# One written order of single-engine pieces in place of two lists and due times: retention, Fourier mixing and a feed-forward block on one NeuronCore

## Chip, cores and metric

The kernel runs on 1 core of one Trainium2 chip. The metric is device time in microseconds (us) of one execution, median of several runs. Three runs of the kernel before took 242.15, 242.26 and 242.28 us.

The core has five engines with a queue of instructions each: TensorE (PE, with its weight loads shown apart as PEld), VectorE (DVE), ScalarE (ACT), GpSimd (POOL) and SyncE (SP). Each engine issues its queue in order. DMA transfers are issued from SP, from POOL (where they also change the type) and now and then from ACT.

## What is computed

Inputs are q, k and v of 4 batches, 8 heads, 768 positions and 64 columns, and two weights of 512 x 2048 and 2048 x 512, all float32.

```python
for t in range(S):                       # retention, per head, with decay gamma
    state = gamma * state + outer(k[t], v[t])
    y[t] = scale * q[t] @ state
x = y, heads side by side                # 768 x 512 per batch
mixed = real(fft(fft(x, axis=1), axis=2))
u = x + mixed
un = (u - mean(u)) / sqrt(var(u) + 1e-6)
out = u + relu(un @ w_ch1) @ w_ch2
```

## The kernel before

**Stages of a batch.** The 768 positions are cut into 6 chunks of 128, the 8 heads into 4 pairs (order 0, 1, 3, 2). For each pair q, k and v (384 KB each) are loaded by SP (L209) into one of 11 input buffers, cast to float16 (L193 and L194 are the helper that records casts and scalings of the first batch; L413 to L428 in later batches), and q and k are transposed: on PE for batches 0 and 1 (products with the identity, L468 and L578, whose results ACT or DVE evict, L584 and L589), by DMA for batches 2 and 3. Then come the scores of each chunk (L492, L622), their masking and decay on DVE (L501, L625), the chunk states (products L516 and L641; the recurrence over the chunks is one scan on DVE in batch 0, L525, and multiply-adds after it, L651), and the outputs (L538 and L548, L672 and L676), which ACT evicts as x (L684).

The real part of the two-dimensional Fourier transform is made by products with cosine and sine tables, folded by their symmetry: DVE adds and subtracts halves (L703, L713), PE does the first axis (L760, L782, L800, L895), ACT and DVE evict g (L767, L771), PE does the second axis (L924, L952, L1006). DVE and POOL add x and the mirrored part to get u (L959 to L991, L1030, L1038), DVE makes the statistics (L1055), ACT the normed un (L1060). un is transposed, either on PE with an eviction (L1105, L1109) or by DMA from SP (L1101). The first product of the feed-forward block writes hidden tiles (L1118, L1135, L1199), relu is their eviction on ACT or DVE (L1122, L1124, L1204), the second product (L1157) is added to u by DVE (L1161) and stored by SP (L1164). In the last batch the second product is made of seven smaller ones of combined blocks (L1270).

The tables are computed on the chip at the start (PE L340 and L343, ACT L359 to L367). The two weights come in four pieces each, w10 to w13 and w20 to w23, 512 KB of float16 each, as casting DMAs on POOL (L1311, L1318).

**What sets the order.** Every step is a Python closure, a unit, with a short name: `k20` casts the first part of pair 2's k, `ae201` masks scores, `sc3` is pair 3's scan, `w10` starts a weight's DMA, `h01` is a hidden product of the first block. Many units of the later batches issue instructions on several engines; for example a transposing unit holds the products of q, their evictions, the products of k and theirs. The order of batch 0's first part is written by hand in the strings FIRST and SECOND. Behind them, `emit` spreads the units of the other work by due times: each stream of units has a start and an end in units of a batch (constants such as DM0, TS0, LD0, HT0), and the units are issued in the order of the times so found.

`pin()` ties each new instruction to the one before it on the same engine, so that the tool that schedules the program keeps that order. It is called for all engines in FIRST, SECOND, in the very first due times and in the last batch. For the rest of batch 0's stretch only POOL's order is pinned, and between them the scheduler may choose. `behind()` and `held()` keep some casts in turn. `late_consts` makes eight scaled copies of the mask on ACT behind one of the first norms.

```python
for e in ev:
    e[3]()
    if e[0] < 1.0:
        behind()
        pin(None if e[0] < 0.05 else ["Pool", "GpSimd"])
    elif e[0] > B - 1:
        pin()
```

A filler (`f512`, L189) is a PE product of zeros, 128 x 512, whose result nobody reads. Eight stand ahead of everything; FIRST holds two more. The loads of batch 0 are issued as q0 k0 v0 q1 k1 v1 q2 k2 q3 k3 v2 v3 at the start, and the weights' DMAs stand in FIRST from `w10`, behind `ae200`, to `w23`. The loads of batch 1 wait for the seventh weight's DMA and a hidden product, those of later batches for score products of the batch before.

Of the kernel before, what the change touches and what calls it, by code (L numbers as in the profile page):

```python
# [18 lines left out]
P = 128  # L19
B, H, S, D = 4, 8, 768, 64  # L20
DM = 512
# [11 lines left out]
DM0, DM1 = (0.120, 0.208, 0.265, 0.344), (0.004, 0.137, 0.232, 0.341)  # L33
TS0 = (0.249, 0.368, 0.406, 0.410, 0.479, 0.544, 0.680, 0.685)
TS1 = (-0.040, -0.020, 0.048, 0.585)
DA0, DA1 = (0.068, 0.080, 0.173, 0.203, 0.292, 0.326), (0.063, 0.067, 0.063, 0.158, 0.168, 0.189)
LD0, LD1 = (0.172, 0.226), (-0.370, 0.140)
HT0 = (0.655, 0.675, 0.673, 0.628)
NPE = 2
LOADS = "q0 k0 v0 q1 k1 v1 q2 k2 q3 k3 v2 v3"  # L40
# [9 lines left out]
FIRST = """  # L50
par qz0 hid hid5 gk3 q0 nid0 ta0 gk1 ta1 gk0 tq0 nid1 gk2 tn0 k00 eq0 tb0 si0 k01 v00 tk0 tn1 ab0
ek00 tb1 co0 ta3 q1 am01 tn3 ab1 am00 tb3 si1 ae000 si3 ta2 ab3 ae010 kv0 co1 ae011 yi00 tn2 sc0
co3 tb2 ab2 tq1 ae001 k10 si2 eq1 k11 co2 nsp tk1 ek10 yi01 v10 yx0 q2 am10 x01 kv1 ae100 am11 x00
sc1 tq2 k20 k21 q3 ae111 eq2 tk2 ae110 tq3 ek20 k30 ae101 am20 am21 ae200 w10 ae201 k31 ae211 yi10
yi11 ae210 yx1 tk3 w11 x10 ek30 eq3 ek31 ta4 w12 tn4 x11 am30 v30 tb4 am31 v20 ae300 stx01 fs0a
w13 si4 f512 kv2 fs0b ab4 yi20 ae301 yi21 co4 cdh0 sc2 v31 s1s10 w20 ae310 yx2 kv3 ae311 x20 s1s00
w21 sc3 x21 yi30 w22 fla yi31 yx3 flb cdh1 x31 w23 fd0 x30 xn1 f512 s1m0 fhb xn0 xm1 stx3 px1 fha
gc00a g0a fd1 s1s11 qe1 xm0 gr0 s1s01 xm2 s1m1 gc11b gc01a xmb gc11a stg00 xe gc01b gc10a stx4 gr3
stg01 g0b gr2 s21 g0c stg10 mu1 qn1 mu2 s22 ul1 stg11 qn2 uu1 stx2 ul2 ste1 gr1 un1 ste0 uu2 xl2
s23 qz1 s20 xu2 qn3 s25 ul3 qn0  # L60
"""
EARLY = (1,)
SECOND = """
h00 un2 ul0 xl3 uu0 xl0 ut1 uu3 h01 xu0 qn5 uu5 s24 xu3 ul5 h10 qn4 un3 xu5 h11 ul4 xl5 uu4 xl4
h12 xu4 ut2 h03 un4 h13 h22 h21 h23 h20 h02
"""
MIX3 = ((0.005, 0.085, 0.110, 0.125, 0.150), (0.190, 0.290, 0.310, 0.325, 0.350),
        (0.345, 0.415, 0.435, 0.460, 0.500))
WS = (0.6, 0.97)
H3_ACT = (0, 1, 2, 3, 5, 6, 7)  # L70
PROD = ((1, 4, 5, 2, 6, 7, 3), (1, 4, 6, 7, 5, 2, 3))
HS_AT = {3: (0, 4), 7: (4, 8)}
# [4 lines left out]
def kernel(  # L77
# [76 lines left out]
    def behind():  # L154
        for x in tc.nc.cur_bb.bb.instructions[mark[0]:]:
            if str(x.engine) in base:
                tc.add_manual_dep(x, base[str(x.engine)],
                                  mybir.DependencyInfo(mybir.DependencyClass.NoSync,
                                                       mybir.DependencyReason.DATA),
                                  reason="behind the first batch")  # L160

    def held(unit):
        def run():
            ins = tc.nc.cur_bb.bb.instructions
            n0 = len(ins)
            unit()
            for n in range(n0, len(ins)):
                m = n - 1
                while m >= 0 and ins[m].engine != ins[n].engine:
                    m -= 1  # L170
                if m >= 0:
                    tc.add_manual_dep(ins[n], ins[m].name,
                                      mybir.DependencyInfo(mybir.DependencyClass.NoSync,
                                                           mybir.DependencyReason.DATA),
                                      reason="casts in turn")
        return run

# [19 lines left out]
    in_of, a_of = {}, {}  # L197
# [3 lines left out]
    def load_unit(b, i, after=None, names="qkv"):  # L201
        def run():
            h0 = 2 * PAIR_ORDER[i]
            for name in names:
                src = srcs[name]
                t = inp.tile([P, 2, NCH, D], f32, tag="in32", name=f"{name}32")
                rows = "h (p c) d -> p h c d" if b < NPE and name == "q" else \
                    "h (c p) d -> p h c d"
                dma = nc.sync.dma_start(t, src[b, h0:h0 + 2].rearrange(rows, p=P))  # L209
                if after is not None:  # L210
                    for x in (w_dma[after].ins, lb[0]["mm"].ins):
                        tc.add_manual_dep(dma.ins, x.name,
                                          mybir.DependencyInfo(mybir.DependencyClass.Sync,
                                                               mybir.DependencyReason.DATA),
                                          reason="loads in turn")
                if b > 1:
                    tc.add_manual_dep(dma.ins, a_of[b - 1, 1].ins.name,
                                      mybir.DependencyInfo(mybir.DependencyClass.Sync,
                                                           mybir.DependencyReason.DATA),
                                      reason="loads behind the transposes")  # L220
                in_of[name, b, i] = t
        return run

    for n in LOADS.split():
        load_unit(0, int(n[1]), names=n[0])()
# [59 lines left out]
    def late_consts():  # L285
        with tc.issue_after(lb[0]["una"].ins):
            for h in range(H):
                nc.scalar.activation(maskp[:, h // 2, h % 2], maskf, AF.Copy, bias=0.0,
                                     scale=float(gam[h] ** (-P)))
# [17 lines left out]
    def pad_unit():  # L307
        for j in range(2):
            nc.vector.memset(qzs[j][:, 0, :, D:P], 0.0)
            nc.vector.memset(qzs[j][:, 1, :, 0:D], 0.0)  # L310

    def qt_zeros():
        for j in range(2):
            nc.vector.memset(qts[j][0:D, 1], 0.0)
            nc.vector.memset(qts[j][D:P, 0], 0.0)
# [85 lines left out]
    def cast_unit(b, i):  # L401
        def run():
            h0 = 2 * PAIR_ORDER[i]
            q32, k32, v32 = (in_of.pop((n, b, i)) for n in "qkv")
            kd = kp.tile([P, NCH, 2, D], f16, tag="kd16", name="kd16")
            v16 = vp.tile([P, NCH, 2, D], f16, tag="v16", name="v16")
            with ExitStack() as es:
                if b < NPE:
                    if (b, i - 1) in last_cast:
                        es.enter_context(tc.issue_after(last_cast[b, i - 1].ins))  # L410
                    q16 = qzs[i % 2].rearrange("p h c d -> p (h c d)")[
                        :, 0:NCH * P].rearrange("p (c h d) -> p c h d", c=NCH, h=2)
                    es.enter_context(tc.issue_after(nc.gpsimd.tensor_scalar(  # L413
                        out=q16, in0=q32.rearrange("p h c d -> p c h d"), scalar1=1.0,
                        scalar2=1.0, op0=ALU.mult, op1=ALU.mult).ins))
                else:
                    q16 = qzs[i % 2]
                    for h2 in range(2):
                        dst = q16[:, h2, :, D * h2:D * h2 + D]
                        nc.gpsimd.tensor_scalar(out=dst, in0=q32[:, h2], scalar1=1.0,  # L420
                                                scalar2=1.0, op0=ALU.mult, op1=ALU.mult)
                for h2 in range(2):
                    kc = nc.gpsimd.tensor_scalar(out=kd[:, :, h2, :], in0=k32[:, h2],  # L423
                                                 scalar1=gkd[:, h0 + h2:h0 + h2 + 1],
                                                 scalar2=1.0, op0=ALU.mult, op1=ALU.mult)
                    if b < NPE:
                        es.enter_context(tc.issue_after(kc.ins))
                last_cast[b, i] = nc.gpsimd.tensor_scalar(  # L428
                    out=v16, in0=v32.rearrange("p h c d -> p c h d"), scalar1=1.0, scalar2=1.0,
                    op0=ALU.mult, op1=ALU.mult)  # L430
            q16_of[b, i], kd_of[b, i], v16_of[b, i] = q16, kd, v16
        return run
# [26 lines left out]
    def t0_unit(i, part):  # L459
        def run():  # L460
            if (0, i) not in at:
                at[0, i] = dict(kT=tp.tile([P, NCH, P], f16, tag="kT", name="kT"),
                                qT=qts[i % 2][:, 0])
# [6 lines left out]

    def te_unit(i, part, n=0):
        def run():
            st = at[0, i]
# [1055 lines left out]
```

## Time and profile before

| What | Value |
|---|---|
| time, median of 3 runs | 242.26 us (242.15 to 242.28) |
| the profiled execution: span from first to last instruction | 240.1 us |
| its time outside the span | the page names none |
| mean granted clock of TensorE | 0.977 |
| PE busy | 231.2 us (96% of the span), 2161 products |
| DVE busy | 189.3 us (79%) |
| ACT busy | 122.2 us (51%) |
| POOL busy | 89.9 us (37%) |
| DMA | 36.41 MB, 152 GB/s on average |

How to read it. A busy time is the sum of the time in which an engine had an instruction under way. PE's products are pipelined, so one that stands in a row of products takes longer from its start to its end than from its start to the next one's start; both are used below and kept apart. In the lines by groups, the columns are the source line, engine, operation, result and inputs, shape and type, count, then busy us and mean ns of one, then the idle time ahead of it and what ended it. In the table of stretches, each engine's busy time stands with its number of instructions, PEclk is the granted clock as a share of full, the DMA share is the sum over queues and can exceed 1. In a timeline the first two columns are start and length in us, and the brackets hold the idle time ahead and its releaser. In the chain of work that ended last, the columns are start, length, and the engine and line. In the slices of the page each digit is a fortieth of the span, 6 us.

### The profile page before, as it was taken

What the parts mean: (1) busy time and instruction counts of PE and PEld (TensorE: products, weight loads), DVE (VectorE), ACT (ScalarE), POOL (GpSimd) and SP (SyncE); (2) the same over time, 40 slices, a digit from 0 to 9 for tenths busy, and PEclk for the clock granted to TensorE, in tenths of its full rate; (3) what the DMA queues carried; (4) which work ended last, traced back from release to release, by engine and by line L of the source; (5) the groups of instructions that cost most, each with busy time, mean ns of one, the idle gap of its engine ahead of it and who ended that gap; (6) DMA issues with size and microseconds to landing.
All of it is one profiled execution on the core that took longest, in us unless ns stands there. A gap on an engine that the chain in (4) does not pass through costs nothing.

```text
span 240.1 us, 5658 instructions
## 1 busy us (share of the span) xinstructions
PE 231.2 (96%) x2161; PEld 159.3 (66%) x2161; DVE 189.3 (79%) x484; ACT 122.2 (51%) x273; POOL 89.9 (37%) x149
## 2 busy tenths in 40 slices
PE   6888899999999999999999999999999999999995
PEld 2465799765765645665567546665567458898884
DVE  7869989877897788996886778899985856777274
ACT  6777775667956345741247423741247316253330
POOL 6667746264400068690000554680000502240302
PEclk9659999999999999999999999999999999999999
DMA  8999999999899647999999558787100141131202
GB/s 175 252 267 195 207 197 201 230 274 248 217 220 215 120 109 164 210 189 144 263 271 212 108 110 227 131 110 171 64 26 0 26 131 44 25 111 25 87 3 87
DMA packets 99466, 36.41 MB, mean 152 GB/s; under 512 B 89840, under 2 KB 96624, under 8 KB 99440
## 3 DMA queue, kind: packets, MB, share of 16 engines
q1 hardware_dynamic: 95072, 31.79, 63.4%
q0 software_dynamic: 4224, 4.19, 10.8%
q8 instruction: 17, 0.28, 0.5%
q14 instruction: 9, 0.07, 0.1%
q10 hardware_dynamic: 144, 0.07, 0.1%
HBM read 27.26 MB, written 6.29 MB: 140 GB/s over the span
## 4 chain that ended last, share of the span: by engine, by line
PE 80%; DVE 6%; ACT 5%; POOL 3%; DMA 2%; issue 2%; SPq 0%; ACTq 0%; POOLq 0%
PE psc L1157 22%; PE psh L1118 19%; PE psh L1199 9%; PE psc L1270 8%; PE psh L1135 4%; PE wkA L622 3%; PE ps L760 3%; PE wkY L676 2%; DMA k<-in_k_dram 2%; PE wkY L672 1%; PE pq L952 1%; ACT qTz L584 1%; PE wkK L641 1%; PE pq L1006 1%; PE tq L468 1%
## 5 line engine op out<-in xcount | busy, mean ns | idle before, releaser
L1157 PE MATMUL psc<-w,ht 128*128 128x512 f16 x288 | 68.5, 379 | 0.0
L1118 PE MATMUL psh<-unT,w 128*128 128x384 f16 x320 | 59.5, 326 | 0.0
L989 POOL TENSOR_TENSOR u<-u,x 128x256 f32<-128x256 f32 x18 | 11.6, 645 | 99.2 <-DVE u L959 98.0
L1157 PEld LDWEIGHTS <-ht 128*128 128x128 f16 x288 | 27.3, 98 | 26.1 <-issue 0.2
L1118 PEld LDWEIGHTS <-w 128*128 128x128 f16 x320 | 29.9, 98 | 16.0 <-issue 0.6
L1122 ACT ACTIVATE ht<-psh 128x384 f16<-128x384 f32 x46 | 22.3, 489 | 23.9 <-PE psh L1118 23.8
L625 DVE TENSOR_TENSOR atm<-wkA,maskp 128x512 f16<-128x512 f32 x36 | 23.9, 685 | 0.7 <-PE wkA L622 0.7
L1199 PE MATMUL psh<-unT,w 128*128 128x256 f16 x192 | 21.5, 272 | 0.0
L1124 DVE TENSOR_SCALAR ht<-psh 128x384 f16<-128x384 f32 x34 | 18.7, 550 | 2.1 <-PE psh L1118 2.0
L1199 PEld LDWEIGHTS <-w 128*128 128x128 f16 x192 | 18.7, 98 | 2.2
L1055 DVE BATCH_NORM_STATS2 bst<-u 128x6 f32<-128x512 f32 x21 | 14.5, 691 | 6.9 <-POOL u L991 6.8
L1204 ACT ACTIVATE ht<-psh 128x512 f16<-128x512 f32 x21 | 12.5, 597 | 12.9 <-PE psh L1199 7.9
L1161 DVE SCALAR_TENSOR_TENSOR ob<-psc,stats,u 128x512 f32<-128x512 f32 x18 | 13.4, 745 | 6.9 <-PE psc L1157 6.7
L651 DVE SCALAR_TENSOR_TENSOR s<-s,gk,wkK 128x128 f16<-128x128 f16 x48 | 16.3, 339 | 1.9 <-ACT s L647 1.3
L684 ACT ACTIVATE x<-wkY,gexp 128x384 f16<-128x384 f32 x24 | 12.8, 581 | 9.7 <-PE wkY L676 9.7
L1060 ACT ACTIVATE un<-u,stats 128x512 f16<-128x512 f32 x15 | 10.8, 720 | 10.7 <-DVE stats L1056 7.7
L423 POOL TENSOR_SCALAR kd<-k,gexp 128x384 f16<-128x384 f32 x24 | 13.9, 588 | 3.1 <-DMA k<-in_k_dram 3.1
L622 PE MATMUL wkA<-qTz,kT 128*128 128x256 f16 x72 | 13.5, 272 | 0.2
L991 POOL TENSOR_TENSOR u<-u,x 128x256 f32<-128x256 f32 x18 | 11.4, 635 | 2.7 <-DVE stats L1056 1.8
L1135 PE MATMUL psh<-unT,w 128*128 128x128 f16 x192 | 11.4, 219 | 0.0
L954 ACT COPY qn<-pq 128x128 f32<-128x128 f32 x18 | 4.9, 274 | 12.4 <-PE pq L952 12.3
L622 PEld LDWEIGHTS <-kT 128*128 128x128 f16 x72 | 6.8, 98 | 6.3 <-ACT kT L589 0.4
(220 smaller groups left out, 432.0 us busy)
## 6 DMA issues: line engine op xcount, KB each, us to landing
q<-in_q_dram SPq DMA_DIRECT2D x16, 384.0 KB, 6.2
k<-in_k_dram SPq DMA_DIRECT2D x16, 384.0 KB, 5.5
v<-in_v_dram SPq DMA_DIRECT2D x16, 384.0 KB, 6.4
out_dram<-ob SPq DMA_DIRECT2D x18, 256.0 KB, 2.8
w<-in_moe_w_ch_dram POOLq DMA_DIRECT2D x8, 512.0 KB, 10.5
out_dram<-o SPq DMA_DIRECT2D x2, 512.0 KB, 2.9
out_dram<-o SPq DMA_DIRECT2D x3, 128.0 KB, 1.7
unT<-un SPq DMA_TRANSPOSE x15, 2.5
```

Source lines behind the costliest of these rows:

```text
L423: kc = nc.gpsimd.tensor_scalar(out=kd[:, :, h2, :], in0=k32[:, h2], scalar1=gkd[:, h0 + h2:h0 + h2 + 1], scalar2=1.0, op0=ALU.mult, op1=AL ...
L622: mm = nc.tensor.matmul(wk[:, c2], st["kT"][:, c, :], st["qT"][:, :, c, :], start=True, stop=True)
L625: nc.vector.tensor_tensor(out=st["atm"][:, 2 * part:2 * part + 2], in0=wk, in1=maskp[:, PAIR_ORDER[i]].unsqueeze(1).to_broadcast([P, 2, 2, ...
L651: nc.vector.scalar_tensor_tensor(out=s16[:, c], in0=s16[:, c - 1], scalar=gk2[:, hp:hp + 1], in1=wk[:, c - c0], op0=ALU.mult, op1=ALU.add)
L1055: nc.vector.bn_stats(bst, u[:, kb, :])
L1118: nc.tensor.matmul(psh, w116[:, cb, fb * P:(fb + 1) * P], unT[:, cb, rt * 384:(rt + 1) * 384], start=(cb == 0), stop=(cb == 3))
L1122: nc.scalar.activation(ht16[:, fb, :], psh, AF.Relu, bias=0.0, scale=-1.0)
L1124: nc.vector.tensor_scalar(out=ht16[:, fb, :], in0=psh, scalar1=-1.0, scalar2=0.0, op0=ALU.mult, op1=ALU.max)
L1135: mm = nc.tensor.matmul(psh[:, f], w116[:, cb, fb * P:(fb + 1) * P], unT[:, cb, kb * P:(kb + 1) * P], start=(cb == 0), stop=(cb == 3))
L1157: nc.tensor.matmul(psc, ht16[:, fb, rb3 * P:(rb3 + 1) * P], w216[:, fb, :], start=(fb == 0), stop=(fb == NFB - 1))
L1199: nc.tensor.matmul(psh[:, t], w116[:, cb, fb * P:(fb + 1) * P], unT[:, cb, p * 256:(p + 1) * 256], start=(cb == 0), stop=(cb == 3))
L1270: nc.tensor.matmul(ps[:, c0:c1], lh(f), rh(f)[:, c0:c1], start=first and f == 0, stop=last and f == 7, skip_group_check=True)
```

## The change

FIRST, SECOND, the due times, `emit`, `behind`, `held` and the many-engine units of later batches go. In their place every unit is cut into pieces that issue on a single engine, and one string, ORDER, of about 1355 names gives the order of all of them, over all four batches:

```diff
-DM0, DM1 = (0.120, 0.208, 0.265, 0.344), (0.004, 0.137, 0.232, 0.341)
...
-LOADS = "q0 k0 v0 q1 k1 v1 q2 k2 q3 k3 v2 v3"
...
-FIRST = """
-par qz0 hid hid5 gk3 q0 nid0 ta0 gk1 ta1 gk0 tq0 nid1 gk2 tn0 k00 eq0 tb0 si0 k01 v00 tk0 tn1 ab0
...
+ORDER = """
+ta1 ta2 nid1 f512 f512 f512 nid0 gk2 lq0 q0 tq0 qtz10 pad11 gk0 lk0 k00 mp6 tn2 tb2 k01 tk0 f512
+gk1 ab2 f512 lv0 v00 qz0 par tn1 lq1 lk1 f512 gk3 f512 si2 lv1 q1 lq2 eq0 ek00 am00 kv0 ae001 k10
+am01 tb1 ab1 k11 tq1 ta3 tn3 ae000 si1 lk2 lq3 v10 ta0 tn0 tb3 ae010 si3 lk3 q2 ab3 tb0 si0 lv2
+f512 f512 f512 tk1 ab0 k21 qtz00 k30 ae011 q3 yi01 w10 sc0 yi00 yx0 eq1 ek10 am11 ae111 x01 tq2
+ae110 am10 ae100 ae101 k20 tk2 eq2 kv1 ek20 am20 sc1 am21 ae211 x00 yi10 yi11 yx1 k31 co1 tk3 x10
+ae210 ae200 ek30 lv3 v20 tq3 eq3 ta4 ae201 tn4 kv2 ek31 hid5 sc2 tb4 am30 f512 ae301 x11 ab4 nsp
+am31 ae300 fs0a fs0b v30 v31 kv3 co4 ae310 w11 si4 yi21 co0 ae311 co3 sc3 yi20 yx2 x20 cdh0 x21
+flb fla fd0 s1s10 yi30 stx01 w12 yi31 yx3 co2 s1s00 s1m0 x30 xn1 stx3 x31 xm0 close fd1 s1m1 fha
+fhb s1s01 g0a hid gc00a s1s11 cdh1 w13 w20 w21 gc10a xmb gc11b stg00 px1 stx4 xn0 mp7 gc01a stg01
...
+1a0_0 1a2_0 1m0_0 1lq2 1tk1 1cv_1 1kv0_1 1m2_0 1s0_1 1s1_0 0h1_5 1s2_1 1cq_2 1tq2 mp2 1ek_1 0h1_3
...
-    for name in FIRST.split():
-        first_of[name]()
-        pin()
...
-    emit(streams)
+    def play(names):
+        for name in names:
+            units[name]()
+            pin()
+
+    units = first_units()
+    pin()
+    play(ORDER.split())
```

The names of a later batch start with its number: `1tk1` transposes k of batch 1's pair 1 on PE, `1ek_1` evicts it, `2dk1` transposes by DMA, `2lk0` loads, `0h1_5` and `0r1_5` are a hidden product and its relu, `0p1_2`, `0o1` and `0st1` are a part of a second product, its addition to u and its store. `pin()` runs behind each piece for all engines, SP and POOL with their DMA queues among them.

Other than the order, three things differ. ORDER holds eleven fillers where FIRST held two, so PE has nine products more; the eight ahead of everything stay. The mask copies of `late_consts` become eight single pieces, `mp0` to `mp7`. And the first weight's DMA waits for the landing of the last load of k in batch 0:

```diff
             w_dma.append(nc.gpsimd.dma_start(
...
+            if g == 0:
+                sync(w_dma[0], load_of["k", 0, 3])
```

In ORDER, `w11` stands behind the casts of the last v (`v30`), and `w12` to `w21` behind a scaling of a table (`cdh0`); on ACT, the cast of pair 2's v (`v20`) stands ahead of the eviction of pair 3's q (`eq3`). The number of instructions on DVE, ACT, POOL and SP is the same in both kernels.

More of the change, by code (lines that the diff above doesn't have):

```diff
@@ L202, in run, with load_piece @@
+    def load_piece(b, i, name):
         def run():
             h0 = 2 * PAIR_ORDER[i]
[L204 to L221, printed above, removed]
@@ L399, with cast_piece @@
     on = dict(x.split(":") for x in ENGINES.split())
-    def cast_unit(b, i):
+    def cast_piece(b, i, what):
         def run():
[L403 to L431, printed above, removed]
@@ new lines, in run, with out3 @@
+            key = ("ps", p, bank_of(p, n), c0)
+            if key not in pr:
+                pr[key] = ps_g.tile([P, 256], f32, tag="g", name="psc", padded_shape=[P, DM])
+            for f in range(f0, f1):
+                nc.tensor.matmul(pr[key][:, c0:c1], lh(f), rh(f)[:, c0:c1],
+                                 start=first and f == 0, stop=last and f == 7,
+                                 skip_group_check=True)
+        return run
+    def out3(p):
+        if "o" not in pr:
+            pr["o"] = up.tile([P, NCH, DM], f32, tag="u32", name="o32")
+        return pr["o"]
```

1023 lines of the change are left out of this document (502 added, 521 removed).

## Prediction

> **What bounds the kernel now.** I read the page's 40 slices first, then a table of stretches, then the chain that ended last inside the two stretches where TensorE (PE) is not full.
>
> ```profile
> PE   6888899999999999999999999999999999999995
> PEclk9659999999999999999999999999999999999999
> PE 80%; DVE 6%; ACT 5%; POOL 3%; DMA 2%; issue 2%; SPq 0%; ACTq 0%; POOLq 0%
> ```
>
> ```profile
> core 0: us, PE busy (x) PEld busy (x) DVE busy (x) ACT busy (x) POOL busy (x), PEclk, DMA share, GB/s
> 0.00:7.50 7.50, 4.92 (x24) 1.97 (x24) 6.09 (x35) 5.16 (x12) 5.17 (x18) 1.00 0.88 192
> 7.50:17.70 10.20, 9.54 (x102) 6.62 (x100) 7.41 (x13) 8.23 (x17) 6.96 (x9) 0.50 1.26 260
> 17.70:30.00 12.30, 10.67 (x167) 8.16 (x165) 11.01 (x29) 9.44 (x23) 8.92 (x13) 1.00 1.24 201
> 30.00:50.00 20.00, 20.00 (x282) 17.20 (x281) 17.84 (x52) 13.66 (x34) 9.47 (x15) 1.00 1.17 218
> 50.00:65.00 15.00, 14.57 (x160) 9.67 (x159) 11.40 (x30) 11.33 (x21) 8.51 (x12) 1.00 1.11 238
> 65.00:85.00 20.00, 19.77 (x183) 12.98 (x182) 16.30 (x41) 11.10 (x23) 0.02 (x1) 1.00 0.94 180
> 85.00:130.00 45.00, 44.55 (x377) 27.66 (x375) 38.39 (x92) 20.25 (x48) 18.90 (x32) 1.00 1.03 200
> 130.00:185.00 55.00, 54.81 (x433) 33.00 (x432) 45.33 (x106) 24.80 (x60) 18.88 (x32) 1.00 0.53 111
> 185.00:237.00 52.00, 52.00 (x451) 41.85 (x450) 35.00 (x90) 18.27 (x43) 13.11 (x18) 1.00 0.18 54
> 237.00:240.10 3.10, 0.32 (x6) 0.14 (x3) 0.56 (x2) 0.00 (x0) 0.00 (x0) 0.91 0.42 137
> ```
>
> PE carries 80% of the chain. It is full from 30 to 50 us and from 185 to 237. So an order of the work can gain in three places only: ahead of 30 us, where PE idles 2.58 + 0.66 + 1.63 = 4.87 us and runs at half clock for 10.2 us; between 50 and 185, where it shows 0.43 + 0.23 + 0.45 + 0.19 = 1.30 us of idle; and in the last 3.1 us, the final eviction and store, which the new order keeps.
>
> The 1.30 us is a lower bound, as a drained pipeline hides its refill behind the last product's modelled end. The chain gives the interval of products in a row:
>
> ```profile
> 48.19 0.22 PE pst L1105 x4
> 48.42 3.88 PE psc L1157 x18
> ...
> 53.15 0.69 ACT qTz L584
> ...
> 57.17 0.81 ACT kT L589
> ```
>
> 3.88 / 18 = 0.216 us for 512 columns, 0.22 / 4 = 0.055 for 128; I take 0.109 for 256 and 0.028 for 64. The products of 51 to 59 us are these:
>
> ```profile
> L1157 PE MATMUL psc<-w,ht 128*128 128x512 f16 x19 | 5.2, 379 | 0.0
> L622 PE MATMUL wkA<-qTz,kT 128*128 128x256 f16 x6 | 1.1, 273 | 0.1
> L641 PE MATMUL wkK<-v,kd 128*128 128x128 f16 x10 | 1.0, 218 | 0.1
> L578 PE MATMUL tq<-ident,q16z 128*128 128x128 f16 x12 | 1.0, 219 | 0.0
> L578 PE MATMUL tq<-ident,kd 128*128 128x128 f16 x12 | 1.0, 218 | 0.2 <-ACT qTz L584 0.2
> L672 PE MATMUL wkY<-s,qTz 128*128 128x64 f16 x10 | 0.6, 193 | 0.0
> ```
>
> With 4 transposes (L1105) and 6 products of L676 more, they need 19 x 0.216 + 6 x 0.109 + 38 x 0.055 + 16 x 0.028 = 7.3 of the 8 us: 0.7 is lost, where the rows show 0.4 of idle. Counted so from the starts of the 1153 products between 50 and 185 us (160 + 183 + 377 + 433 in the table), the loss is about 1.4 us until 65 and 3.3 after it.
>
> **The change part by part.** The page names no time for the profiled execution beside its span of 240.1 us; against the median of 242.26 us, 2.16 us lie around it, and I keep them. Both versions issue the same work on DVE, ACT, POOL and SP; PE gets nine more products. So the terms are waits.
>
> *Nine products without a result.* Their kind in the trace:
>
> ```profile
> L189 PE MATMUL wps<-ht x10: 379/620/634, 1.2 to 26.4; 128*128 128x512 f16 x10
> ```
>
> Warm they cost 9 x 0.216 = 1.9 us of PE; cold, at twice that, 3.9. Ten of the eleven in the new list stand ahead of the third pair's state, where PE idles and waits for loads and casts; I take 0, as the 4.87 us of idle cover them. If that cover goes they cost up to 3.9.
>
> A gain from them would have to come through the clock: at 0.50 the 9.54 us of PE work between 7.5 and 17.7 us would shrink to 4.8 at full clock. The Trainium skill, "TensorE: Matmul & The Clock Gate", section "Part 1: The HAM clock gate", says that the array runs at half rate after an idle window of some 3.4 us and returns to full rate after one busy window. By that rule fillers ahead of 7.5 us keep the clock up. The trace speaks half for it: the clock falls behind a stretch with 2.58 us of idle, but it stays at 0.50 for 10.2 us although PE shows 94% busy. I count no gain from it in the sum, and keep it as a rival.
>
> *First weights behind the third k, the others behind the last v.* The rows ahead of the end of the first batch's attention, on POOL, ACT and DVE, and the bytes of 18.5 to 22.4 us by queue (q0 are POOL's weights):
>
> ```profile
> 18.59 2.46 POOL L1311 DMA_DIRECT2D w<-in_moe_w_ch_dram  x3
> 22.55 0.56 POOL L194 TENSOR_SCALAR v<-v 128x384 f16<-128x384 f32 x1 [1.50 <-DMA v<-in_v_dram]
> ```
> ```profile
> 20.04 0.80 ACT L193 ACTIVATE qTz<-tq 128x768 f16<-128x768 f16 x1
> ...
> 21.19 0.85 ACT L193 ACTIVATE v<-v 128x768 f16<-128x768 f32 x1
> ```
> ```profile
> 23.13 0.81 DVE L525 TENSOR_TENSOR_SCAN s<-gk,wkK 128x320 f16<-128x320 f32 x1
> 23.86 0.99 DVE L501 SCALAR_TENSOR_TENSOR atm<-wkA,maskf 128x384 f16<-128x384 f32 x2
> 24.96 0.82 DVE L525 TENSOR_TENSOR_SCAN s<-gk,wkK 128x320 f16<-128x320 f32 x1
> 25.70 0.61 DVE L703 TENSOR_TENSOR xab<-x 128x390 f16<-128x390 f16 x2
> ...
> 26.78 0.54 DVE L713 TENSOR_TENSOR eo<-xab 128x768 f16<-128x768 f16 x1
> ```
> ```profile
> q1 hardware_dynamic: 1852, 0.47, 72.3%
> q0 software_dynamic: 258, 0.26, 49.0%
> ```
>
> Weights took 0.26 of 0.73 MB while v2 and v3 were under way, 36% of 3.9 us: without them v3 lands 1.4 us earlier, with w10 alone in front about 0.7 earlier, at 21.8. That is not gained whole. On ACT the cast of v2 (0.85) now stands ahead of the eviction of the fourth pair's q (0.80), which before was done at 20.84: with v2 at about 20.4 (its cast started at 21.19 before), that eviction ends at 22.0, 1.2 late, and the fourth pair's masked products on DVE follow it. In exchange DVE's scan of pair 2 comes at 21.6 instead of 23.13. Behind that scan's end at 22.4 the list holds seven DVE pieces: four masked products and two folds at about 0.46 from start to start (two in 0.99 with the last one's tail), and the last scan (0.82), 3.5 us: it ends at 25.9, before at 25.78. Then come the small folds (0.61) and the difference (0.54) at once, where before a table's scaling of 0.6 stood between them: 27.0 instead of 27.32, so the first Fourier products start 0.3 us earlier. Behind them PE's list counts: PE still idles 1.63 us between 17.7 and 30, and the new order brings Fourier products and small transposes of later use into it; of these 1.63 us I take 0.7. **Sum of the start: -1.0 us**, bounds +0.9 (the 1.2 of the late eviction less the 0.3) and -3.0 (all of the 1.63, and v3 with no weights in front, 1.4).
>
> The lower bound comes from the weights. By 30 us the table of stretches has moved 7.5 x 192 + 10.2 x 260 + 12.3 x 201 = 6.6 MB; the twelve loads are 12 x 393 KB = 4.7 of these, so 1.9 MB are weights, and the fourth piece of 0.52 MB has passed near 31 us. The new list asks for it in its second hidden product, some 2 us behind the point where PE is full. It is late next if the start gains 2 or more.
>
> *Batch 1's transposes and evictions, 50 to 65 us.* Before, the chain runs over ACT's evictions from 53.15 to 57.98 (the quoted first and last of six, each 0.7 to 0.8, with a copy between them), with PE short of ready products. The new list puts two hidden products of 16 x 0.055 and three second products of 4 x 0.216 between the transposes of pair 0 and their first use: 1.8 + 2.6 = 4.4 us of PE work over three evictions of 0.8, a copy and a norm of 0.7 (3.3 us). The cover is there, so most of the 1.4 us goes: **-1.0**, bounds 0 and -1.4.
>
> *Everything pinned to single-engine pieces, 65 to 185 us.* An instruction that the scheduler put at a busy engine's tail can now stand where it is wanted; each engine, SP's and POOL's queues too, waits in the written order. No row shows which of 3.3 us stays. I take a bit less than half, **-1.5**; bounds -3.3 and +8 (the slower rival). What is late next are the Fourier folds on DVE (16.30 of 20 us busy in 65 to 85), which feed PE with about 1 us to spare.
>
> *185 us on, and the tail:* PE is full before; 0.
>
> Sum: 240.1 - 1.0 - 1.0 - 1.5 = 236.6 us span, and with 2.16 around it **238.8 us**.
>
> **The rivals.**
>
> *The clock stays up.* Then the start gains its bound of 3.0 instead of 1.0: 238.8 - 2.0 = 236.8 us. For it: the fillers fall into the idle of the first 7.5 us, and the clock falls just behind it. Against it: DVE (11.01 of 12.3 us busy in 17.7 to 30) and the loads pace this part. Chance 0.13.
>
> *Part of it only.* The order trades old waits for new ones of the same size in one half of the kernel: the start gains nothing (late eviction) and the later gaps give 1.2: 241.1 us. Chance 0.12.
>
> *Slower: SP's queue as a line in which all wait.* Where loads, stores and DMA transposes stand in one written order, a load whose buffer is still held, or a store whose result is late, holds the transposes behind it, and PE has nothing else that its own list lets it do.
>
> ```profile
> v<-in_v_dram SPq DMA_DIRECT2D x16, 384.0 KB, 6.4
> ...
> unT<-un SPq DMA_TRANSPOSE x15, 2.5
> ```
>
> Of the 31 transposes on SP in the new list (15 of them the norm's) 15 follow directly on a load or a store, 11 in the old list. If PE stands for 8 of these for about 1 us (2.5 less the cover), 8 us come in. With the start and the stretch until 65 us still gained (-2.0) and no gain in the later part the time is 242.26 - 2.0 + 8 = 248.3 us, with half of that wait 244.3. It decides from 2 us, a quarter of a microsecond per transpose held. I put the case at 244.3. For it: the lists were not free to move when a wait lasts longer than in this trace. Against it: PE has several products between the transposes and their use, and the loads, at a median of 6.4 us, are issued further ahead than that. Chance 0.25.
>
> *The order changes, the time doesn't:* if loads and DVE pace the start and the later waits are data and not order, 242.3 us. Chance 0.05.
>
> **How the numbers follow.** Forecast (238 to 240 us) 0.45, clock 0.13, part 0.12, slower 0.25, same 0.05. Within 0.2% is about what a measurement of this kernel can tell from no change. So faster 0.70, same 0.05, slower 0.25. The range goes from the clock rival with the gaps' full gain in part (236.8 - 1.2 = 235.6) to just short of the slower case's middle, 244.0, which leaves out half of that case (0.13) and some 0.05 below.
>
> **What would show it.** Right: the cast of the last v on POOL starts before 22 us; the last scan on DVE ends near 25.9; the first Fourier products start near 27.0; PE idle between 50 and 65 us under 0.2; no row of waits on PE for the transposed norm. Wrong: a PEclk row without the 5 and 6 (the clock rival); PE idle above 1.3 us between 65 and 185, ended by unT or by folds (the slower one); the fillers at the head of the chain ahead of the first transposes of q; eviction of the fourth q later than 22 us with DVE idle behind it.

## The result and the profile after

The changed kernel takes 239.83 us (median of 6 runs, 239.21 to 241.16); the kernel before took 242.2 us in the same comparison (6 runs, 241.99 to 243.46). The ratio is 0.990, interval 0.988 to 0.993: 1% faster, 2.4 us. The profiled execution took 239.83 us with a span of 238.1 us, 1.7 us around it; before, the span was 240.1 us. So 2.0 us of the gain lie in the span. The rest lies around it: in the executions of the kernel before for which both numbers are listed, 2.0 to 2.2 us stand around the span, in those of the changed kernel 1.7 to 1.8. No run shows what shortened it; the hybrid below, with the old start, has 2.0 to 2.1 again.

The slices of PE and its clock and the shares of the chain, from the page of the changed kernel:

```profile
PE   7777979999999999999999999999999999999994
PEclk9999999999999999999999999999999999999999
PE 83%; DMA 8%; SPq 5%; DVE 1%; issue 1%; POOL 1%; ACT 0%; POOLq 0%
```

The 5 and the 6 of the clock are gone. (The row says nothing of the first 5 us; see a_nofill.) DVE's and ACT's shares of the chain (6% and 5% before) went to 1% and 0%; DMA's rose from 2% to 8%. The table of stretches says where:

```profile
core 0: us, PE busy (x) PEld busy (x) DVE busy (x) ACT busy (x) POOL busy (x), PEclk, DMA share, GB/s
0.00:7.50 7.50, 5.54 (x23) 1.98 (x24) 5.84 (x34) 5.41 (x13) 4.89 (x17) 1.00 0.87 188
7.50:17.70 10.20, 8.08 (x116) 4.94 (x116) 7.59 (x15) 6.52 (x13) 5.05 (x7) 1.00 1.26 260
17.70:30.00 12.30, 10.96 (x173) 8.60 (x168) 11.49 (x31) 10.98 (x25) 8.89 (x13) 1.00 1.08 168
30.00:50.00 20.00, 18.51 (x243) 15.24 (x242) 15.78 (x47) 12.05 (x29) 8.90 (x14) 1.00 1.16 201
50.00:65.00 15.00, 15.00 (x165) 10.78 (x163) 11.86 (x26) 10.66 (x19) 9.44 (x14) 1.00 1.17 241
65.00:85.00 20.00, 20.00 (x215) 14.15 (x214) 17.80 (x45) 13.95 (x32) 4.91 (x10) 1.00 1.27 200
85.00:130.00 45.00, 44.85 (x383) 28.51 (x381) 40.95 (x95) 21.44 (x50) 21.40 (x36) 1.00 1.13 201
130.00:185.00 55.00, 55.00 (x447) 33.89 (x445) 46.78 (x108) 23.61 (x60) 16.05 (x26) 1.00 0.52 106
```

Between 50 and 185 us PE shows 0.15 us of idle instead of 1.30. Between 30 and 50, where it had none, it now shows 1.49. All of that is one wait, the only one of PE's that the view of waits shows behind 25 us:

```profile
PE psh L1128 <- DMA w<-in_moe_w_ch_dram: 1.5, 1, 1.5
```

The table of losses, with one profile of each kernel, counts the loss as the prediction did: from each product's start to the next start, less the interval of its width (0.216 us for 512 columns, 0.162 for 384, 0.109 for 256, 0.056 for 128, 0.029 for 64). "Useful at 35" is the sum of these intervals of the products that started before 35 us, without the fillers of the lists. Each row is one execution; that of the hybrid and that of a_spfree are about 1 us faster than the median of their runs.

| kernel | lost 0-35 | 35-50 | 50-65 | 65-185 | useful at 35 | span |
|---|---|---|---|---|---|---|
| before | 12.5 | 0.0 | 1.4 | 3.3 | 20.8 | 240.1 |
| changed | 11.8 | 0.0 | 0.0 | 1.2 | 19.6 | 238.1 |
| changed, again | 11.1 | 0.0 | 0.0 | 1.3 | 20.3 | 237.5 |
| a_nofill | 14.1 | 0.4 | 0.0 | 1.6 | 19.3 | 239.1 |
| a_h03 | 10.6 | 0.5 | 0.7 | 1.8 | 20.9 | 238.6 |
| a_h03_nofill | 14.6 | 0.4 | 0.0 | 1.3 | 18.7 | 239.6 |
| b_fill | 12.4 | 0.0 | 1.3 | 3.9 | 19.1 | 242.4 |
| a_wearly | 12.2 | 0.0 | 0.0 | 1.3 | 19.3 | 238.5 |
| a_wearly_h03 | 12.0 | 0.5 | 0.0 | 1.5 | 19.4 | 239.1 |
| a_w2 | 10.9 | 0.0 | 0.0 | 1.0 | 20.5 | 237.0 |
| a_w2_h03 | 10.9 | 0.4 | 0.0 | 2.3 | 20.5 | 238.7 |
| hybrid | 13.0 | 0.7 | 0.5 | 0.9 | 20.3 | 237.9 |
| a_spfree | 11.1 | 0.0 | 0.0 | 1.9 | 20.3 | 238.0 |
| a_free | 11.2 | 0.0 | 2.6 | 5.6 | 20.2 | 246.7 |

So from before to changed: behind 50 us 3.5 us are gained; at 35 us the changed kernel is 20.8 - 19.6 = 1.2 us behind; the tail behind the last product grew from 2.8 to 3.1. 3.5 - 1.2 - 0.3 = 2.0, which is 240.1 - 238.1.

**How 50 to 65 us became full.** PE in the changed kernel, from the timeline:

```profile
51.81 0.50 PE L596 MATMUL tq<-ident,q16z 128*128 128x128 f16 x6
52.14 0.50 PE L596 MATMUL tq<-ident,kd 128*128 128x128 f16 x6
52.48 0.39 PE L1088 MATMUL pst<-ident,un 128*128 128x128 f16 x4
52.70 1.95 PE L1128 MATMUL psh<-unT,w 128*128 128x128 f16 x32
...
54.71 0.44 PE L643 MATMUL wkK<-v,kd 128*128 128x128 f16 x5
54.99 2.75 PE L1146 MATMUL psc<-w,ht 128*128 128x512 f16 x12
57.58 0.38 PE L620 MATMUL wkA<-qTz,kT 128*128 128x256 f16 x2
```

Between the transposes of pair 0 and their first use (L620) stand 5.1 us of products that need nothing of them, and ACT's evictions of 0.8 run beside them. Before, at 52.56 to 57.98 the evictions were the chain.

**The start.** DVE's scans and ACT's eviction of the fourth q, and POOL's queue:

```profile
20.04 0.84 ACT L223 ACTIVATE v<-v 128x768 f16<-128x768 f32 x1
20.79 0.79 ACT L223 ACTIVATE qTz<-tq 128x768 f16<-128x768 f16 x1
```
```profile
21.44 0.82 DVE L534 TENSOR_TENSOR_SCAN s<-gk,wkK 128x320 f16<-128x320 f32 x1
...
24.97 0.81 DVE L534 TENSOR_TENSOR_SCAN s<-gk,wkK 128x320 f16<-128x320 f32 x1
```
```profile
19.77 0.94 POOL L1298 DMA_DIRECT2D w<-in_moe_w_ch_dram  x1
...
22.48 0.51 POOL L224 TENSOR_SCALAR v<-v 128x384 f16<-128x384 f32 x1 [0.30 <-DMA v<-in_v_dram]
22.94 0.81 POOL L1298 DMA_DIRECT2D w<-in_moe_w_ch_dram  x1
24.63 0.61 POOL L224 TENSOR_SCALAR ht<-cd 128x512 f16<-128x512 f16 x1 [0.89 <-DVE atm L510]
25.20 1.54 POOL L1298 DMA_DIRECT2D w<-in_moe_w_ch_dram  x2
```

v2 could be cast at 20.04 (21.19 before), but the last v came no earlier: its cast starts at 22.48, before at 22.55. The last scan ends at 25.78, to the hundredth as before. The second weight piece is issued at 22.94, the third and fourth from 25.20, where before three were issued by 21.05; the transfers moved 168 GB/s between 17.7 and 30 us instead of 201, and the fourth piece, issued at 25.99, landed at 34.81.

### The profile page after: what moved, and what is told of

Its sections match the earlier page's. It is cut to its first block, busy times and chain, and to the rows that moved or that the text cites. A ratio compares the mean times of both kernels' runs of the same rounds, so it can differ in the third digit from the quotient of the medians.

```text
span 238.1 us, 5639 instructions
## 1 busy us (share of the span) xinstructions
PE 227.9 (96%) x2170; PEld 158.4 (67%) x2170; DVE 192.4 (81%) x484; ACT 121.2 (51%) x273; POOL 90.4 (38%) x149
## 4 chain that ended last, share of the span: by engine, by line
PE 83%; DMA 8%; SPq 5%; DVE 1%; issue 1%; POOL 1%; ACT 0%; POOLq 0%
PE psc L1146 25%; PE psh L1106 22%; PE psh L1192 9%; PE psc L1242 8%; SPq L244 5%; PE psh L1128 4%; DMA w<-in_moe_w_ch_dram 4%; PE wkA L620 3%; DMA v<-in_v_dram 3%; PE ps L767 3%; PE pq L950 2%; PE wkY L679 2%; DMA kT<-kd 1%; PE wkK L643 1%; PE wkY L670 1%; PE tq L596 1%
## 5 line engine op out<-in xcount | busy, mean ns | idle before, releaser
L1146 PE MATMUL psc<-w,ht 128*128 128x512 f16 x288 | 67.2, 379 | 0.0
L988 POOL TENSOR_TENSOR u<-u,x 128x256 f32<-128x256 f32 x36 | 22.2, 639 | 58.9 <-DVE u L978 51.1
L1106 PEld LDWEIGHTS <-w 128*128 128x128 f16 x320 | 30.0, 98 | 16.2
L1201 ACT ACTIVATE ht<-psh 128x512 f16<-128x512 f32 x21 | 12.3, 597 | 20.4 <-PE psh L1192 19.3
L1192 PE MATMUL psh<-unT,w 128*128 128x256 f16 x192 | 22.5, 273 | 0.0
L224 POOL TENSOR_SCALAR kd<-k,gexp 128x384 f16<-128x384 f32 x30 | 17.3, 584 | 11.5 <-DMA k<-in_k_dram 9.7
L224 POOL TENSOR_SCALAR q16z<-q 128x384 f16<-128x384 f32 (+1 forms) x24 | 15.3, 646 | 14.9 <-DMA q<-in_q_dram 14.9
L1192 PEld LDWEIGHTS <-w 128*128 128x128 f16 x192 | 18.8, 98 | 2.4
L1043 DVE BATCH_NORM_STATS2 bst<-u 128x6 f32<-128x512 f32 x24 | 16.4, 684 | 2.0 <-POOL u L1033 1.2
L1280 POOL TENSOR_TENSOR u<-u,ws 128x256 f32<-128x256 f32 (+1 forms) x6 | 5.7, 977 | 32.3 <-DVE u L1280 17.2
L224 POOL TENSOR_SCALAR v<-v 128x768 f16<-128x768 f32 (+1 forms) x15 | 12.1, 809 | 13.6 <-DMA v<-in_v_dram 13.6
L1128 PE MATMUL psh<-unT,w 128*128 128x128 f16 x192 | 12.2, 219 | 1.5 <-DMA w<-in_moe_w_ch_dram 1.5
L1128 PEld LDWEIGHTS <-w 128*128 128x128 f16 x192 | 11.3, 98 | 2.2 <-DMA w<-in_moe_w_ch_dram 1.7
```

What stands on the lines that cost most here:

```text
L224: return (nc.gpsimd if e == "P" else nc.vector).tensor_scalar(out=out, in0=in_, scalar1=scale, scalar2=1.0, op0=ALU.mult, op1=ALU.mult)
L988: nc.gpsimd.tensor_tensor(out=u[:, lo:hi], in0=u[:, lo:hi], in1=x[:, 1, 257:1:-1] if n else x[:, 0, 1:257], op=ALU.add)
L1043: nc.vector.bn_stats(bst, lb[b]["u"][:, kb, :])
L1106: nc.tensor.matmul(psh, w116[:, cb, fb * P:(fb + 1) * P], lb[b]["unT"][:, cb, rt * 384:(rt + 1) * 384], start=(cb == 0), stop=(cb == 3))
L1128: mm = nc.tensor.matmul(psh[:, f], w116[:, cb, fb * P:(fb + 1) * P], unT[:, cb, kb * P:(kb + 1) * P], start=(cb == 0), stop=(cb == 3))
L1146: nc.tensor.matmul(lb[b]["psc", rb], ht16[:, fb, rb % 3 * P:rb % 3 * P + P], w216[:, fb, :], start=(fb == 0), stop=(fb == NFB - 1))
```

## The experiments

Runs on different chips are compared by their ratio to the kernel before on the same chip, which took 242.2 to 243.4 us in the median; its single executions range from 242.0 to 244.4, so differences of a few tenths of a per cent between ratios mean little. The labels with a_ are edits of the changed kernel, b_ of the kernel before.

### a_nofill: two fillers instead of eleven

```diff
-ta1 ta2 nid1 f512 f512 f512 nid0 gk2 lq0 q0 tq0
+ta1 ta2 nid1 nid0 gk2 lq0 q0 tq0
...
-am30 f512 ae301
+am30 f512 ae301
...
-s1s00 s1m0
+s1s00 f512 s1m0
```

> The changed kernel with two fillers in its list instead of eleven, at the places that the old list had them. Theory A (the gain lies behind 50 us, the start is paced by loads, DVE and the weights): the clock falls to 0.50 for some 10 us again, PE still waits for the fourth weight piece at about 34.8, and the time stays at 239.8 within 0.5. Theory B (the gain is the clock that the fillers keep): the 8.1 us of PE work between 7.5 and 17.7 take longer, the last scan on DVE ends 1 to 2 us later than 25.8, and the time is 241 to 242.

240.98 us, ratio 0.993 (0.991 to 0.995). It lies above the changed kernel (0.990, and 0.986 in the later run, below) by 0.7 to 1.6 us; the interval overlaps that of the first of the two. Theory B is the nearer one, though most of the gain on the kernel before, about 1.7 us, is left without the fillers. The products between 7.5 and 17.7 us, first without the nine fillers, then of the changed kernel:

```profile
L499 PE MATMUL wkA<-qTz,kT 64*128 64x128 f16 x24 | 2.0, 301 | 1.1 <-DVE kT L222 0.7 <-DVE qTz L222 0.4
L475 PE MATMUL tq<-ident,kd 128*128 128x128 f16 x12 | 1.9, 312 | 0.0
```
```profile
L501 PE MATMUL wkA<-qTz,kT 64*128 64x128 f16 x32 | 1.8, 219 | 0.9 <-ACT kT L223 0.5 <-DVE qTz L224 0.4
L477 PE MATMUL tq<-ident,kd 128*128 128x128 f16 x18 | 1.5, 219 | 0.7 <-POOL kd L224 0.7
```

301 and 312 ns against 219: without the fillers the products run slow, and the last scan on DVE ends at 27.64 us, 1.9 later than in the changed kernel:

```profile
26.83 0.81 DVE L532 TENSOR_TENSOR_SCAN s<-gk,wkK 128x320 f16<-128x320 f32 x1
```

This execution's row of the granted clock shows 1.00 all the same. The row is made of the clock's records in the trace, and here the first of them begins at 20.78 us; what lies ahead of it is shown as 1.00 because nothing is recorded. In the first profile of the changed kernel the records begin at 5.04 us and in the second at 9.90. Up to there the fillers take up to 634 ns, behind it 377 to 390. So what differs between these executions is when the full speed comes, and in the new order the last scan follows it:

| profile of the new order | full clock recorded from | last scan ends |
|---|---|---|
| changed | 5.04 | 25.78 |
| a_w2 | 5.42 | 25.84 |
| a_h03 | 9.48 | 26.17 |
| changed, again | 9.90 | 26.38 |
| a_nofill | 20.78 | 27.64 |
| a_h03_nofill | 25.08 | 28.29 |

(In a_h03_nofill the clock is also full from 4.60 to 8.01 us.) PE then loses 14.1 us by 35 in a_nofill instead of 11.8 or 11.1. The nine products cost 1.9 us of PE and save 2.3 to 2.9: their worth is about a microsecond, and it comes through the speed of the others.

### a_h03: the product that needs the fourth weight piece moved back

```diff
-s22 h01 h03 qn2 ul2 mp1 uu2 gr0 s23 qn3 uu3 h02 ut1 te1 h00 qtz11
+s22 h01 qn2 ul2 mp1 uu2 gr0 s23 qn3 uu3 h02 ut1 te1 h00 h03 qtz11
```

> The changed kernel with the hidden product that needs the fourth weight piece (h03) moved from second to fourth place of its block. Theory A (PE stands 1.5 us for that piece, and the same work is ready behind it): PE's wait of 1.49 us near 33.4 goes, the time falls by 1.2 to 1.5, to 238.4. Rival: the next piece or DVE's u takes its place, and the time stays at 239.8 within 0.4.

240.23 us, ratio 0.990 (0.986 to 0.993): no gain. The wait for the piece is gone and the kernel is 0.6 to 1.3 us ahead at 35 us, and all of it is given back: 0.5 before 50, 0.7 before 65 and 0.5 more behind. The chain of this run just behind 50 us shows how:

```profile
43.25 7.05 DMA k<-in_k_dram
...
50.39 1.16 POOL kd L223 x2
51.55 0.61 POOL u L1032
...
52.18 0.71 DVE bst L1042
...
53.21 0.72 ACT un L1054
...
53.96 0.81 ACT kT L610
...
54.81 0.27 PE wkK L642 x2
```

POOL's list has the casts of batch 1's k ahead of an addition to u of batch 0. The load of that k lands at 50.30, where it landed at 50.00 and 49.38 in the two profiles of the changed kernel; the addition, the statistics, the norm on ACT and the eviction behind it all wait for it. PE's lead does not bring it earlier: the loads of batch 1 start 0.15 us behind the landing of the seventh weight piece, which the code makes them wait for (42.64 and 42.79 here, 43.20 and 43.35 in the changed kernel). This is how 0.7 us were given back in this execution. The three other profiles with h03 moved lose nothing between 50 and 65 us; they lose 0.4 to 0.5 before and 1.3 to 2.3 behind.

### a_h03_nofill: both

> Both edits: h03 later and two fillers instead of eleven. Theory A (loads and DVE pace the start whatever the clock): the same as with h03 moved alone, within 0.4, so 238.4. Theory B (the clock counts as soon as the weights do not hide it): 1 to 2 us above that run, 239.5 to 240.5.

241.45 us, ratio 0.995 (0.992 to 0.997), 1.2 us above a_h03 on the same chip. Theory B's direction and, nearly, its size: the nine fillers are worth about 1 us with h03 in either place.

### b_fill: nine fillers in the kernel before

```diff
-ta0 gk1 ta1 gk0 tq0
+ta0 gk1 ta1 f512 f512 f512 gk0 tq0
...
-k01 v00 tk0 tn1
+k01 v00 tk0 f512 f512 f512 f512 tn1
...
-co2 nsp tk1
+co2 nsp f512 f512 tk1
```

> The kernel before with nine fillers added to its first list ahead of pair 1's transposes, eleven in all. Theory A: the clock stays at 1.00, the last scan on DVE still ends near 25.8, the time stays at 242.2 within 0.4. Theory B: the start gains what the clock is worth, 240.2 to 241.2. Against both: the fillers stand in the way of ready products, up to 1.9 us more, 244.

244.38 us, ratio 1.006 (1.003 to 1.008): slower by 1.4 us, worked out from the ratio. In the old order, at these places, fillers do harm: the third expectation, against both theories. The last scan on DVE ends at 27.68 us instead of 25.78. The stretches of this run:

```profile
7.50:17.70 10.20, 8.40 (x106) 5.31 (x104) 7.37 (x13) 8.04 (x18) 6.37 (x9) 1.00 1.26 261
17.70:24.00 6.30, 5.07 (x81) 3.36 (x81) 5.78 (x14) 5.26 (x10) 4.80 (x7) 0.94 1.18 188
24.00:30.00 6.00, 5.65 (x78) 4.34 (x78) 4.72 (x12) 3.23 (x8) 4.06 (x6) 0.78 1.25 207
```

The clock is at 1.00 where it was at 0.50 (its records begin at 9.62 us here), but falls to a mean of 0.78 between 24 and 30 us, where before it was full and where the Fourier products begin: it is at half from 23.27 to 26.68 us, behind 3.41 us in which PE was busy for 2.64. The loss by 35 us is that of the kernel before (12.4 against 12.5), with 1.9 us of fillers on top: the useful work at 35 us is 1.7 less.

### a_wearly and a_w2: the weights earlier

```diff
-ae011 q3 yi01 w10 sc0
+ae011 q3 yi01 w10 w11 w12 sc0
```

> The changed kernel with the second and third weight piece issued directly behind the first, ahead of v2 and v3's casts, as the old list had them. Theory C (in the changed kernel the transfers up to 66 us follow one another without a break, and the late weights put 3 us of idle into them at the start): the fourth piece lands near 32.7 instead of 34.8, PE's 1.5 us of wait for it goes, the loads of batch 1 land 2 us earlier, v3 still lands near 22.4, and the time is 1.0 to 1.5 below the changed kernel: 0.985 of the kernel before. Rival D (the late weights buy an earlier v3): v3 lands 1 later, the last scan on DVE ends near 26.8 and the time stays, 0.990.

240.14 us, ratio 0.987 (0.984 to 0.990): the changed kernel's own time within the intervals. PE's wait for the piece went, the loads of batch 1 did not come earlier (the last v at 66.7 us, 66.3 in the changed kernel), and the clock fell to 0.86 between 17.7 and 30 us in the profiled run. The last v landed at 22.42 us, as in the changed kernel, but the three issues, 2.45 us on POOL's queue, held its cast back to 23.62. The fall of the clock spoils the test of theory C: it is at half from 25.22 to 28.63 us, behind 3.41 us in which PE was busy for only 1.49, and all four executions show a mean clock of 0.984 to 0.993, where nine of the twelve of the changed kernel show 0.998 or more. So in a_w2 the third piece stands behind that cast:

```diff
-ae011 q3 yi01 w10 sc0
+ae011 q3 yi01 w10 w11 sc0
...
-v30 v31 kv3
+v30 w12 v31 kv3
```

> The changed kernel with the second weight piece directly behind the first and the third directly behind the cast of the last v, ahead of the table's scaling. With both pieces ahead (the earlier run) POOL came to that cast 1 us late; here it should start near 22.7. Theory C (the weights' late issue is what the start loses): PE's wait for the fourth piece near 33 falls from 1.5 to under 0.3 us, nothing behind 35 us changes, 0.985 of the kernel before, 1.2 us less than the changed kernel. Rival (clock): the wait goes, but PE idles in other places ahead of 30 us and the executions with a lower clock eat it: 0.988 to 0.990.

> The changed kernel once more, beside the other runs of this call: 0.990 of the kernel before, with executions whose mean clock is below 0.99 about 1.5 us longer than those at 1.00.

239.02 us, ratio 0.985 (0.982 to 0.989), beside 239.38 us, 0.986 (0.983 to 0.990), for the changed kernel itself on the same chip. (The mean clock does not order the executions as expected: one at 0.983 took 239.67 us, the longest, 241.08, shows 1.00. The mean goes by the same records and leaves out a slow start ahead of the first.) PE's wait was 0.3 us in a_w2, but in the second profile of the changed kernel it was also short:

```profile
PE psh L1127 <- DMA w<-in_moe_w_ch_dram: 0.3, 1, 0.3
```
```profile
PE wkA L620 <- DMA kT<-kd: 0.3, 1, 0.3
PE psh L1128 <- DMA w<-in_moe_w_ch_dram: 0.2, 1, 0.2
```

The 1.5 us were thus one execution's share of a wait that is mostly shorter: the fourth piece landed at 34.12 here instead of 34.81. Theory C is not borne out as a cause of 1 us or more. No run is clearly better than the changed kernel; a_w2 has the lowest median.

The same weights with h03 moved gave nothing either:

> The same with h03 moved from second to fourth place too. Theory C: with the weights early nothing waits for the fourth piece any more, so as the run with the weights early alone within 0.3 us, 0.985. If h03 moved alone failed for a reason on PE or DVE and not for transfers that come at their time anyway, this run shows the same gaps at 40 to 45 and 50 to 65 us again, 0.990.

241.03 us, 0.992 (0.990 to 0.995), with 0.5 us lost between 35 and 50 us again, but nothing between 50 and 65.

> The same weights, and h03 in fourth place. Theory H (moving h03 only changes which wait comes: DVE's u and POOL's casts of batch 1 come at their own time): the same as with the weights alone or 0.3 us above, 0.985 to 0.987. If h03's place was good and only the late weights spoiled it: 0.983.

239.75 us, 0.987 (0.984 to 0.991), with 0.4 us lost between 35 and 50 us. Moving h03 back gained nothing in any of four pairs: with the changed kernel, without the fillers, and with either place of the early weights.

### hybrid: the old start, then the new list

FIRST and SECOND of the kernel before, in their order, with the new pieces for the norm and its transposes; then what is left of ORDER, in its order. In effect:

```diff
-    play(ORDER.split())
+    first = LOADS + FIRST + SECOND          # names in the old order
+    play(first + [n for n in ORDER.split() if n not in first])
```

> Batch 0's first part in the order of the old two lists (two fillers, weights early), then the rest of the new list; all engines pinned. Theory A (the change gains behind 50 us and loses at the start): the start is that of the kernel before, PE dense from 30 us, and the gaps between 50 and 185 us stay below 1.5 us: 236.7 us of span, 0.986 of the kernel before. Rival E (the later part only fits to its own start): gaps of 2 us and more come back behind 50 us, 0.990 to 0.997.

241.19 us, ratio 0.993 (0.990 to 0.997). Behind 50 us the profiled execution loses 0.5 + 0.9 us, where the kernel before loses 4.7, so the later list keeps most of its gain with another start. But the old start does not bring the 1.2 us: PE's waits behind 30 us in this run,

```profile
PE psh L1126 <- DVE unT L222: 0.6, 1, 0.6
PE psh L1126 <- DVE unT L1093: 0.5, 1, 0.5
PE wkK L641 <- DVE unT L1093: 0.3, 1, 0.3
```

are evictions of the transposed norm on DVE, where the two orders meet. Neither theory fits whole: the ratio is rival E's, but its gaps of 2 us and more behind 50 us did not come (1.4, and 0.7 between 35 and 50).

### a_free and a_spfree: fewer engines pinned

In a_free the pieces are issued in the same sequence, but from the first second product (0p0_0) on only POOL's order is pinned, as the kernel before had it for batch 0's stretch.

```diff
         for name in names:
             units[name]()
-            pin()
+            late = late or name == "0p0_0"
+            pin(["Pool", "GpSimd"] if late else None)
```

> The changed kernel with its pieces issued in the same order, but from the first second product on only POOL is pinned, so that the scheduler may move DVE's, ACT's and SP's instructions (it keeps PE's nearly as they are). Theory F (the written order across all engines removes the waits): gaps between 50 and 185 us grow from 1.3 to over 3 us, 0.998 of the kernel before. Rival G (the cut into pieces and their sequence do it, the pin adds nothing): as the changed kernel, 0.990.

249.01 us, ratio 1.024 (1.020 to 1.028): 3.4 to 3.8% above the changed kernel and 2.4% above the kernel before, more than theory F had it. PE's own order is all but the same; what it waits for is the eviction that DVE or ACT put behind something else:

```profile
PE psh L1128 <- ACT ht L1135: 1.8, 1, 1.8
PE psh L1192 <- DVE ob L1153: 1.7, 2, 1.0
PE psc L1146 <- DVE ht L1117: 1.6, 1, 1.6
PE wkA L620 <- DMA qTz<-q16z: 1.5, 1, 1.5
```

Here is the first of them, in the chain:

```profile
49.93 1.15 POOL kd L224 x2
51.09 0.61 POOL u L1033
...
52.75 0.72 ACT un L1055
53.47 0.49 ACT ht L1135
...
54.00 2.04 PE psh L1128 x31
```

On ACT a norm that waits for POOL stands ahead of an eviction that is ready, and PE stands for a free PSUM tile. In the changed kernel ACT stands idle ahead of neither norm of this stretch (49.80 and 53.16 us). So this order needs the pins. What they would do for the old order stays open: no run pins that one on all engines.

In a_spfree all engines are pinned but SP:

```diff
+            pin(["PE", "Pool", "DVE", "Act"] if late else None)
```

> The changed kernel with SP's queue left to the scheduler from the first second product on, all other engines pinned as before; the scheduler then moves some ten transposes, loads and stores against each other. The prediction's slower rival (SP's written queue holds transposes behind loads): the time falls below 0.988. Theory F2 (SP's written order costs nothing here): 0.990 or, where a transpose now comes late, 0.992 to 0.998.

240.6 us, ratio 0.990 (0.986 to 0.993), beside 0.986 (0.983 to 0.990) for the changed kernel on the same chip. The intervals overlap: no gain shows, and at most a small loss. Its profile shows one wait that the changed kernel has not:

```profile
PE wkA L620 <- DMA qTz<-q16z: 0.9, 1, 0.9
```

A transpose of q that the scheduler put behind others. SP's written order costs nothing that can be seen.

## Why the prediction held, point by point

**The time.** 238.8 us were forecast, 239.83 came; 3.5 us of gain against 2.4. The direction and the two later terms hold; the start had the wrong sign. That the sum is only 1.0 off owes something to luck, as errors cancel: the start came 2.2 us worse than forecast and the tail, put at 0, 0.3 worse; 50 to 185 us gave 1.0 more and the time around the span 0.4 more.

**50 to 65 us, -1.0 forecast: -1.4.** The trace shows the mechanism as it was argued: products that need nothing of the transposes now cover ACT's evictions. It takes all of the loss, the bound that the prediction gave. No experiment moves these products alone.

**65 to 185 us, -1.5 forecast: -2.1** (3.3 to 1.2 lost). The term was a guess between ends far apart, and came out larger. a_free shows that it needs pins beside POOL's: the same pieces without them lose 8.2 us behind 50 us instead of 1.2. a_spfree shows that SP's pin carries little or none, which leaves those of DVE and ACT, as PE's order hardly changes. How much the cut into pieces, the order and the pins each give is not separated.

**The start, -1.0 forecast: +1.2 in the first profile, +0.5 in the second.** This is the step that failed. Its parts: the last scan was put at 25.9 and came at 25.78, but with the clock full from 5.04 us, which the forecast did not count on; it came at 26.4 in the second profile and at 27.6 without the fillers, so that agreement is luck. The eviction of the fourth q, at 22.0, came at 21.58; the Fourier products from 27 us on run in a row, as said. But the last v was put at 21.8, 0.7 earlier for having one weight piece ahead of it instead of three, and its cast came at 22.48. The share of bytes that weights had in that time (36%) was taken as time that v would save; it was not. At 30 us the changed kernel is 0.4 us ahead in the first profile (16.2 of useful products against 15.8) and 0.1 behind in the second. Then come the weights: named as "late next if the start gains 2 or more", they were late without it, since the edit that was to free v3 issued them up to 5 us later (the third piece at 25.20 instead of 20.30); PE waits 1.5 us for the fourth in the first profile, 0.2 in the second.

**The fillers, 0 forecast.** By PE's count they add 1.9 us, all in the start; a_nofill and a_h03_nofill show that they bring that back and 0.7 to 1.6 us more. The cover that the prediction named (idle time) is not what pays: the speed of the other products is.

**The clock rival, 236.8 us.** Half of it came: the products of 7.5 to 17.7 us ran at 219 ns instead of 306. Its time did not. The reason that was held against it, that DVE and the loads pace this part, does not hold as it stands: in the new order the last scan comes later the later the full speed comes (25.78 to 28.29 in the table under a_nofill). The new order with fast products only reaches the 25.78 that the old one reaches with slow ones. By the rule of the Trainium skill, "TensorE: Matmul & The Clock Gate", section "Part 1: The HAM clock gate", the clock is throttled by default and activity releases it. The changed kernel agrees (products of 631 ns up to 5 us, then full speed). The other half of this rule of the Trainium skill, half rate after an idle window of some 3.4 us, does not agree with b_fill, where PE was busy for 2.64 of the 3.41 us ahead of the fall.

**The slower rival, SP's queue.** Not seen: PE waits for no transpose in the first profile, for one of 0.3 us in the second, and a_spfree is not faster.

What stays open: why v3 landed at the same time with one weight piece ahead of it as with three, what the wait of the first weight for k3 is worth by itself, as no run leaves it out alone, and how far the start's gain or loss is a matter of the execution (1.2 or 0.5 us behind at 35 in two of them).

## What to carry to other kernels

When one engine is nearly full, time that is won ahead of a load can be given back there if the load waits for something other than that engine: look for the next load, and for the instruction that stands behind its cast on the same queue, before you count it. An order written for one engine is only as good as the order of the engines that evict for it: the same sequence of pieces was 2.4% slower than the old kernel with only POOL pinned, and 1% faster with all of them. Count a filler by the speed of the products behind it, in the order in which it stands: nine of them were worth about 1 us in one order and cost 1.4 us in the other.

## What was not expected of the hardware

The row of the granted clock shows 1.00 where the trace has no record of the clock, and ahead of the first record the products were slow in every profile here: in a_nofill, where it begins at 20.78 us, 128-column products took 301 to 312 ns, as long as those of the kernel before at a recorded 0.50, and 219 ns in the changed kernel. So too the fillers ahead of everything: in the kernel before, with a first record at 4.05 us, seven of the eight took 517 to 634 ns, the eighth 380. The mean duration of one shape in a stretch is the safer reading.

A load's share of the bytes did not tell when it lands: with one weight piece under way or three, the last v landed within 0.1 us of the same time (22.41 and 22.47), and in all other profiles but one (21.62, with three) between 22.4 and 22.8. The v ahead of it came 1.1 us earlier (20.02 and 21.13), but not for the number of pieces: a_wearly, with three, has 20.02 as well. What its order shares with the changed kernel is the later issue of the first piece, 19.76 and 19.77 against 18.59.
